# Small sums on GpSimd, attention evictions on ScalarE and two weight sums joined, in a fused attention and two-stage feed-forward kernel

## The chip, the cores and the metric

The kernel runs on one core of one Trainium2 chip. The metric is the device time of one execution in microseconds. Of the kernel before there are three timed runs and one profiled execution.

## What is computed

Three stages follow each other, all in fp32 accuracy:

```
scores = q @ k.T / sqrt(64) + alibi bias, masked to 0 <= i - j < 128
attn   = exp(scores - max) ; attn / (sum(attn) + 1e-9)     # per row
x      = attn @ v, heads side by side                      # [2304, 512]
x      = (sigmoid(x @ w_gate) * (x @ w_val)) @ w_out       # 512 -> 1536 -> 512
expert = argmax(normalised x @ normalised expert_emb.T)    # 8 experts, one each token
out    = gate * (relu(x @ w1[expert]) @ w2[expert])
```

There are 4 batches of 8 heads with 576 rows of 64. An fp32 product is made of three matmuls of split operands (high and low parts), which is why so many copies and subtractions stand beside the matmuls.

## The kernel before

The attention is cut into 36 *units*: a pair of heads on 256 rows. Five engines work on several units at once, each on its own queue, in order:

- `unit_s(i)`: TensorE writes the scores of unit i to two PSUM banks. In `tail`, VectorE reduces each of four pieces of 128x192 (line 229: adds the bias, takes the maximum) and ScalarE makes the exp of each piece with its row sum in `su` (line 232). Pieces at the ends of a sequence use an edge tile for the bias, which `make_edge` has GpSimd compute (line 160).
- `unit_n(i)`: a small instruction on 128x4 adds 1e-9 to the four sums (line 247, tile `rs`), VectorE takes the reciprocals (line 248), and GpSimd scales the four pieces with them (line 111).
- `unit_t(i)`: TensorE transposes the scaled pieces (line 261), ScalarE and VectorE copy them out (`tt`).
- `unit_b(i)`: TensorE multiplies by v (lines 283 and 289, "AV"); the two halves of 128x128 are copied from PSUM to `xf` (line 296, the eviction).

Step i of the loop issues `unit_t(i)`, `unit_b(i-1)`, `unit_n(i+2)`, `make_edge(i+5)`, `unit_s(i+3)`. Up to step 9 (`SPLIT`) TensorE, VectorE, ScalarE and GpSimd keep exactly this order; from step 10 to 20 only TensorE and GpSimd do, and a scheduler sets the order on VectorE and ScalarE; from unit 20 on all four are again in written order, and the first feed-forward stage runs between the units' pieces.

That stage takes its weights in blocks f = 0 to 11 and multiplies with seven products in place of eight for a 2x2 split (`seven`), for which `sum_x` and `sum_w` add and subtract quarters. `sum_w(f)` makes T1 = b12 - b11 and T3 = b12 - b22 (lines 363 and 364), then T2 and T4 (lines 366 and 367) on VectorE, from a block of 128 x (4 quarters of 2x128). `split_x` casts an input to its high part on ScalarE and subtracts it on VectorE (128x1024). The weights come as 64-bit words, and `conv64_a` and `conv64_b` convert them.

```python
        for i in range(SPLIT):
            if i < NA:
                unit_t(i)
            if i:
                unit_b(i - 1)()
                load_v(i + 3)
            if i < NA:
                unit_n(i + 2)
                for t in AB.get(i, []):
                    t()
                make_edge(i + 5)
                unit_s(i + LEAD)
```

Of the kernel before, what the change touches and what calls it, by code (L numbers as in the profile page):

```python
# [15 lines left out]
ALU = mybir.AluOpType  # L16
# [11 lines left out]
P = 128  # L28
# [21 lines left out]
NA = 20  # L50
# [7 lines left out]
def attn_ffn_moe(ctx: ExitStack, tc: tile.TileContext, qkd, vd, wgv, w_out, emb, tau, w1, w2, cst, ids, out):  # L58
    nc = tc.nc
# [21 lines left out]
    def slot(shape, dt, name):  # L81
        return bpool.tile(shape, dt, tag="b", name=name)
# [14 lines left out]
    def hi_copy(eng, o, i):  # L97
        if eng == "a":
            nc.scalar.copy(o, i)  # L99
        elif eng == "v":  # L100
            nc.vector.tensor_copy(o, i)
        else:
            nc.gpsimd.tensor_scalar(out=o, in0=i, scalar1=1.0, scalar2=0.0, op0=ALU.mult, op1=ALU.add)

    def scale_rows(eng, t, r):
        if eng == "a":
            nc.scalar.mul(t, t, r)
        elif eng == "v":
            nc.vector.tensor_scalar_mul(t, t, r)
        else:  # L110
            nc.gpsimd.tensor_scalar(out=t, in0=t, scalar1=r, scalar2=0.0, op0=ALU.mult, op1=ALU.add)  # L111
# [129 lines left out]
    def unit_n(i):  # L241
        if i >= NU or i in has_n:
            return
        has_n.add(i)
        p, su = fst[i]
        rs = ap.tile([P, 4], F32, tag="rs", name=f"rs{i}", bufs=4)
        nc.vector.tensor_scalar_add(rs, su, 1e-9)
        nc.vector.reciprocal(out=rs, in_=rs)  # L248
        for u in range(2):
            for j in range(2):  # L250
                scale_rows("p" if i >= 2 else "vp"[j], p[:, u, j, :], rs[:, 2 * u + j:2 * u + j + 1])
# [17 lines left out]
    def x_of(c, b, g):  # L269
        b0, nb = chunks[c]  # L270
        per = 1024 // (nb * P)
        if g % per == 0 and b == b0:
            xf[c, g // per] = slot([P, per, nb * P], F32, f"xf{c}_{g}")
        return xf[c, g // per][:, g % per, (b - b0) * P:(b - b0) * P + 256]

    def unit_b(i):
        c, b, g = units[i]
        tts, os = fst.pop(i)
        v = v_t.pop(i)
        for j in range(2):  # L280
            for u in range(2):
                c0 = j * 2 * P
                nc.tensor.matmul(os[j][u * D:u * D + D, :], v[:, j, u * D:u * D + D], tts[u][:, c0:c0 + P],
                                 start=True, stop=False, skip_group_check=True)
        for y in range(2):
            for j in range(2):
                rows, m = slice(j * 64, j * 64 + 64), 2 if j == y else 1 - j
                for u in range(2):
                    nc.tensor.matmul(os[j][u * D:u * D + D, y * 64:y * 64 + 64], v[rows, m, u * D:u * D + D],
                                     tts[u][rows, P + y * 64:P + y * 64 + 64], start=False, stop=True,  # L290
                                     skip_group_check=True)
        x = x_of(c, b, g)

        def evict():
            for j in range(2):
                hi_copy("v" if i < 11 or j and i < NA else "a", x[:, j * P:(j + 1) * P], os[j])

        return evict

# [36 lines left out]
    def flat(t):  # L336
        return t.rearrange("p a f -> p (a f)")
# [18 lines left out]
    def sum_w(f, part="01"):  # L356
        if f < KF:
            if "0" in part:
                tf[f] = slot([P, 2 * KD, P], F32, f"tf{f}")
            w, t = wf[f], tf[f]  # L360
            b11, b21, b12, b22 = (w[:, 2 * z:2 * z + 2] for z in range(4))
            if "0" in part:
                nc.vector.tensor_tensor(out=t[:, 0:2], in0=b12, in1=b11, op=ALU.subtract)
                nc.vector.tensor_tensor(out=t[:, 4:6], in0=b12, in1=b22, op=ALU.subtract)
            if "1" in part:
                nc.vector.tensor_tensor(out=t[:, 2:4], in0=b22, in1=t[:, 0:2], op=ALU.subtract)
                nc.vector.tensor_tensor(out=t[:, 6:8], in0=b21, in1=t[:, 2:4], op=ALU.subtract)
                nc.sync.dma_start(tf_d[f * P:(f + 1) * P, :], flat(t))
# [138 lines left out]
    def latest(*engines):  # L507
# [6 lines left out]
        5: [lambda: split_x("rest", xf[0, 0], "h")], 6: [lambda: split_x("rest", xf.pop((0, 0)), "l")],  # L514
        12: [bA["S1+"]], 13: [bA["A22"], lambda: load_w(0)], 14: [bA["S1"], lambda: conv_w(0, 0)],
        15: [lambda: conv_w(0, 1), lambda: load_w(1)], 16: [lambda: sum_w(0)],
        17: [bA["A11"], lambda: split_w(0, 0, 0)], 18: [bA["S3+"], lambda: split_w(0, 0, 1)],
        19: [bA["S3"], bA["S2+"], sA[0]["rg"]], 20: [bA["S2"], sA[0]["rv"]],
    }
    AB = {}  # L520
    with tc.manual_schedule(engines={ENG.PE, ENG.DVE, ENG.Activation, ENG.Pool}):
# [14 lines left out]
        load_qk(4)  # L536
        load_qk(5)
        unit_n(0)
        unit_s(2)
        keep_warm(6)  # L540
        load_qk(6)
        unit_n(1)
# [12 lines that stand above are left out]
                load_qk(i + LEAD + 4)  # L555
            for t in AT.get(i, []):
                t()
# [20 lines left out]
    def bulk(f):  # L578
        return {
            0: [lambda: load_w(f + 2), lambda: conv_w(f + 1, 0, "a")],  # L580
            1: [lambda: conv_w(f + 1, 1, "a"), lambda: conv_w(f + 1, 0, "b")],
            2: [lambda: conv_w(f + 1, 1, "b")],
            3: [lambda: split_w(0, f + 1, 0, "h"), lambda: sum_w(f + 1, "0")],
            4: [lambda: sum_w(f + 1, "1")],
            5: [lambda: split_w(0, f + 1, 0, "l")],
            6: [lambda: split_w(0, f + 1, 1, "h")],
            7: [lambda: split_w(0, f + 1, 1, "l")],
        }
# [120 lines left out]
    for f in range(KF):  # L709
        s, t = sv[f], sv[f + 1] if f + 1 < KF else None  # L710
# [528 lines left out]
```

## Time and profile before

| | |
|---|---|
| median of three runs | 831.67 us (831.55 to 832.48) |
| the profiled execution, its own time | 831.14 us |
| its span, first to last instruction | 829.4 us |
| TensorE matmuls busy | 802.5 us (97%) |
| VectorE busy | 548.6 us (66%) |
| ScalarE busy | 447.5 us (54%) |
| GpSimd busy | 176.8 us (21%) |

The profile is of one execution. Engines are named as on its page: PE is TensorE (PEld its weight loads), DVE VectorE, ACT ScalarE, POOL GpSimd, SP the queue that issues most DMAs. In a timeline a row is one instruction, or several equal ones that follow each other; in square brackets stands how long the engine had been idle before it, and what ended that. Durations overlap a little with the next instruction's start, so the spacing of starts is the better price of a short one. TensorE's busy time covers matmuls that were issued and were still waiting for something inside, so it is not time at the peak.

### The profile page before, as it was taken

What the parts mean: (1) busy time and instruction counts of PE and PEld (TensorE: products, weight loads), DVE (VectorE), ACT (ScalarE), POOL (GpSimd) and SP (SyncE); (2) the same over time, 40 slices, a digit from 0 to 9 for tenths busy, and PEclk for the clock granted to TensorE, in tenths of its full rate; (3) what the DMA queues carried; (4) which work ended last, traced back from release to release, by engine and by line L of the source; (5) the groups of instructions that cost most, each with busy time, mean ns of one, the idle gap of its engine ahead of it and who ended that gap; (6) DMA issues with size and microseconds to landing.
All of it is one profiled execution on the core that took longest, in us unless ns stands there. A gap on an engine that the chain in (4) does not pass through costs nothing. (4 is left out here: it accounts for less than half of the span.)

```text
span 829.4 us, 15487 instructions
## 1 busy us (share of the span) xinstructions
PE 802.5 (97%) x5597; PEld 657.0 (79%) x5598; DVE 548.6 (66%) x1385; ACT 447.5 (54%) x943; POOL 176.8 (21%) x263
## 2 busy tenths in 40 slices
PE   8988799999999999999999999999999999999996
PEld 5766587888888788887777777778778988978885
DVE  6999877777788888878555545547745545545443
ACT  6888666766555666568455554435334433424331
POOL 5877332322100000000010000131322030230210
PEclk9999999999999999999999999999999999999999
DMA  7686655645456486667144445142565554453510
GB/s 261 186 250 194 218 190 195 233 155 190 160 191 208 156 279 230 225 237 227 51 136 144 141 145 155 69 141 52 179 213 177 188 177 129 150 203 120 180 69 18
DMA packets 67568, 141.45 MB, mean 171 GB/s; under 512 B 8440, under 2 KB 28664, under 8 KB 67490
## 3 DMA queue, kind: packets, MB, share of 16 engines
q1 hardware_dynamic: 63586, 130.32, 48.2%
q0 software_dynamic: 3904, 10.12, 3.7%
q8 instruction: 45, 0.74, 0.4%
q14 instruction: 33, 0.27, 0.1%
HBM read 104.14 MB, written 36.93 MB: 170 GB/s over the span
## 5 line engine op out<-in xcount | busy, mean ns | idle before, releaser
L801 PE MATMUL y<-wo,gh 128*128 128x512 f32 x432 | 141.2, 402 | 0.0
L981 PE MATMUL h<-xe,weh 128*128 128x256 f32 (+4 forms) x512 | 105.9, 301 | 1.4 <-DVE h L984 1.4
L111 POOL TENSOR_SCALAR p<-p,rs 128x192 f32<-128x192 f32 x140 | 81.1, 596 | 103.5 <-DVE rs L248 49.0
L997 PE MATMUL z<-weh,h 128*128 128x512 f32 (+3 forms) x320 | 103.1, 399 | 0.0
L801 PEld LDWEIGHTS y<-wo,gh 128*128 128x128 f32 x432 | 79.9, 188 | 20.4 <-issue 3.3
L115 DVE TENSOR_TENSOR wel<-wer,weh 128x1024 fp32r<-128x1024 f32 x64 | 78.1, 1223 | 19.9 <-ACT weh L99 18.8
L981 PEld LDWEIGHTS h<-xe,weh 128*128 128x128 f32 x512 | 83.2, 188 | 4.2 <-DVE h L984 2.9
L801 PE MATMUL y<-wo,gl 128*128 128x512 f32 x216 | 85.8, 398 | 0.0
L983 ACT ACTIVATE h<-h 128x256 fp32r<-128x256 f32 (+4 forms) x64 | 26.6, 418 | 95.5 <-PE h L981 91.9
L232 ACT ACTIVATE p<-p,mx 128x192 f32<-128x192 f32 x144 | 64.1, 447 | 25.0 <-DVE mx L229 24.3
L981 PE MATMUL h<-xe,wel 128*128 128x256 f32 (+4 forms) x256 | 76.2, 299 | 0.3 <-DVE wel L115 0.2
L99 ACT CAST weh<-wer 128x1024 fp32r<-128x1024 f32 x64 | 66.2, 1048 | 8.7 <-DMA wer<-in_w 8.7
L997 PEld LDWEIGHTS z<-weh,h 128*128 128x128 f32 (+3 forms) x320 | 56.6, 180 | 15.0
L997 PE MATMUL z<-wel,h 128*128 128x512 f32 (+3 forms) x160 | 63.1, 395 | 0.0
L1002 POOL DMA_INDIRECT out<-y,cols x19 | 24.9, 1311 | 172.0 <-DVE y L1001 161.1
L1001 DVE TENSOR_SCALAR y<-z,xg 128x512 f32<-128x512 f32 (+3 forms) x22 | 16.5, 749 | 57.5 <-PE z L997 50.3
L984 DVE SCALAR_TENSOR_TENSOR h<-h,h 128x256 fp32r<-128x256 f32 (+4 forms) x64 | 29.6, 464 | 37.6 <-ACT h L983 37.3
L895 POOL DMA_INDIRECT tab_d<-ids_sb,ai x18 | 18.3, 1017 | 162.0 <-DVE ai L892 142.4
L817 ACT ACTIVATE xr<-y 128x512 f32<-128x512 f32 x18 | 10.8, 598 | 76.2 <-PE y L801 68.9
L981 PEld LDWEIGHTS h<-xe,wel 128*128 128x128 f32 x256 | 48.0, 188 | 0.7 <-DVE wel L115 0.7
L801 PEld LDWEIGHTS y<-wo,gl 128*128 128x128 f32 x216 | 40.5, 188 | 9.0
L822 DVE COPY xT<-tl 128x512 f32<-128x512 f32 x18 | 12.5, 692 | 41.5 <-PE tl L821 41.5
(332 smaller groups left out, 1940.3 us busy)
## 6 DMA issues: line engine op xcount, KB each, us to landing
wer<-in_w SPq DMA_DIRECT2D x64, 512.0 KB, 4.5
gl<-gT_d SPq DMA_DIRECT2D x27, 512.0 KB, 5.6
wr<-in_wgv SPq DMA_DIRECT2D x24, 512.0 KB, 5.2
gT_d<-c SPq DMA_DIRECT2D x48, 256.0 KB, 2.2
qk<-in_qkd SPq DMA_DIRECT2D x36, 320.0 KB, 3.4
v<-in_vd SPq DMA_DIRECT2D x36, 192.0 KB, 2.6
wf_d<-wf SPq DMA_DIRECT2D x12, 512.0 KB, 2.8
tf_d<-tf SPq DMA_DIRECT2D x12, 512.0 KB, 3.2
```

The lines of the kernel that those rows point to most:

```text
L99: nc.scalar.copy(o, i)
L111: nc.gpsimd.tensor_scalar(out=t, in0=t, scalar1=r, scalar2=0.0, op0=ALU.mult, op1=ALU.add)
L115: e.tensor_tensor(out=o, in0=i, in1=h.bitcast(F32), op=ALU.subtract)
L232: nc.scalar.activation(out=o, in_=o, func=AF.Exp, scale=-1.0, bias=mx[:, z:z + 1], accum_out=su[:, z:z + 1])
L801: nc.tensor.matmul(m, g[:, k % 4, u * P:(u + 1) * P], w[:, k % 3, :], start=(k == 0 and z == 0), stop=(k == KF - 1 and z == 2))
L895: nc.gpsimd.indirect_dma_start(out=tab_d, out_offset=IOA(ap=ai[:, u:u + 1], axis=0), in_=ids_sb[:, t:t + 1], in_offset=None)
L981: nc.tensor.matmul(m[:, :n], w[:, fs], x[:, k, :], start=(cnt == 0), stop=(cnt == 3 * KD - 1))
L983: nc.scalar.activation(out=hh, in_=m[:, :n], func=AF.Relu)
L984: nc.vector.scalar_tensor_tensor(out=hl, in0=m[:, :n], scalar=0.0, in1=hh.bitcast(F32), op0=ALU.max, op1=ALU.subtract)
L997: nc.tensor.matmul(m[0:w, :], h, ww[:, ds], start=(cnt == 0), stop=(cnt == 3 * KE - 1))
L1001: nc.vector.tensor_scalar_mul(y[0:w, :], m[0:w, :], x[0:w, DM:DM + 1])
L1002: nc.gpsimd.indirect_dma_start(out=out, out_offset=IOA(ap=idx[0:w], axis=0), in_=y[0:w, :], in_offset=None, bounds_check=NT - 1, oob_is_er ...
```

## The change

Three edits. The small sum of `unit_n` goes from VectorE to GpSimd, for all 36 units. The eviction of `unit_b` is on VectorE only for the second half (j = 1) of units 0 to 10; it was on VectorE for both halves of these and for the second half of units 11 to 19. The rest of them are on ScalarE. And `sum_w` makes T1 and T3 in one instruction of 128x512 elements, with b12 read twice, in place of two of 128x256.

```diff
@@ unit_n
         rs = ap.tile([P, 4], F32, tag="rs", name=f"rs{i}", bufs=4)
-        nc.vector.tensor_scalar_add(rs, su, 1e-9)
+        nc.gpsimd.tensor_scalar(out=rs, in0=su, scalar1=1e-9, scalar2=0.0, op0=ALU.add, op1=ALU.add)
         nc.vector.reciprocal(out=rs, in_=rs)
@@ unit_b
             for j in range(2):
-                hi_copy("v" if i < 11 or j and i < NA else "a", x[:, j * P:(j + 1) * P], os[j])
+                hi_copy("v" if j and i < 11 else "a", x[:, j * P:(j + 1) * P], os[j])
@@ sum_w
             if "0" in part:
-                nc.vector.tensor_tensor(out=t[:, 0:2], in0=b12, in1=b11, op=ALU.subtract)
-                nc.vector.tensor_tensor(out=t[:, 4:6], in0=b12, in1=b22, op=ALU.subtract)
+                w4, t4 = (y.rearrange("p (b k) c -> p b k c", b=4) for y in (w, t))
+                nc.vector.tensor_tensor(out=t4[:, 0::2], in0=w4[:, 2:3].broadcast_to([P, 2, 2, P]), in1=w4[:, 0::3],
+                                        op=ALU.subtract)
```

GpSimd's queue around unit 3, before (p_224, p_289 and p_352 are the pieces of units 2, 3 and 4; edge_0_269 and edge_2_272 the edge tiles of unit 5, edge_0_400 and edge_2_403 those of unit 7):

```order
L111 TENSOR_SCALAR p_224<-p_224,rs_262 128x192 x4
L160 TENSOR_SCALAR edge_0_269<-relm 128x192 x2
L160 TENSOR_SCALAR edge_2_272<-relm 128x192 x2
L111 TENSOR_SCALAR p_289<-p_289,rs_331 128x192 x4
L111 TENSOR_SCALAR p_352<-p_352,rs_393 128x192 x4
L160 TENSOR_SCALAR edge_0_400<-relm 128x192 x2
L160 TENSOR_SCALAR edge_2_403<-relm 128x192 x2
```

and after the change, from the edges of unit 5 on:

```order
L160 TENSOR_SCALAR edge_2_272<-relm 128x192 x2
L247 TENSOR_SCALAR rs_331<-su_291 128x4
L111 TENSOR_SCALAR p_289<-p_289,rs_331 128x192 x4
L247 TENSOR_SCALAR rs_393<-su_354 128x4
L111 TENSOR_SCALAR p_352<-p_352,rs_393 128x192 x4
L160 TENSOR_SCALAR edge_0_400<-relm 128x192 x2
L160 TENSOR_SCALAR edge_2_403<-relm 128x192 x2
L247 TENSOR_SCALAR rs_461<-su_422 128x4
```

Each sum stands right ahead of its unit's scaling, and for units 3, 5, 7 and so on behind the edges of a later unit.

VectorE's queue around the reciprocal of unit 17, in the part that the scheduler orders, before (xl_(0, 'S1') is the low part of a feed-forward input, rs_1258 the small tile of unit 17, tt_1_1237 the transposed pieces of unit 15, xf_0_1109 the attention's output):

```order
L115 TENSOR_TENSOR xl_(0, 'S1')_1222<-xq_(0, 'S1')_1083,xh_(0, 'S1')_1221 128x1024
L101 COPY xf_0_1109<-t_1_1162 128x128
L247 TENSOR_SCALAR rs_1258<-su_1210 128x4
L101 COPY tt_1_1237<-t_1_1236 128x384
L125 TENSOR_SCALAR wf_1225<-wf_1225 128x512
L248 RECIPROCAL rs_1258<-rs_1258 128x4
L229 ISA p_1279,mx_1280<-s_0_1265,bias_130 128x192
```

and after:

```order
L115 TENSOR_TENSOR xl_(0, 'S1')_1222<-xq_(0, 'S1')_1083,xh_(0, 'S1')_1221 128x1024
L248 RECIPROCAL rs_1258<-rs_1258 128x4
L101 COPY tt_1_1237<-t_1_1236 128x384
L125 TENSOR_SCALAR wf_1225<-wf_1225 128x512
L229 ISA p_1279,mx_1280<-s_0_1265,bias_130 128x192
```

The eviction and the sum are gone, and the reciprocal, which now waits for GpSimd, has moved ahead of the copy and the conversion.

## Rows read from the trace of the kernel before

**Rows 1.** Windows by stretch: span, then busy us of each engine, clock, DMA.

```profile
16.00:47.00 31.00, 29.70 (x622) 24.55 (x626) 28.09 (x146) 26.06 (x104) 25.98 (x66) 1.00 0.68 192
47.00:78.00 31.00, 25.27 (x447) 19.55 (x438) 29.51 (x114) 26.18 (x90) 22.82 (x41) 1.00 0.77 246
78.00:100.00 22.00, 17.73 (x165) 13.53 (x164) 19.51 (x44) 15.65 (x43) 9.80 (x13) 0.99 0.56 182
210.00:400.00 190.00, 189.48 (x949) 156.21 (x948) 157.84 (x234) 116.47 (x179) 1.50 (x3) 1.00 0.62 211
```

**Rows 2.** Timeline of VectorE, units 3, 4 and 13: start us, us, engine, line.

```profile
17.27 0.18 DVE L248 RECIPROCAL rs<-rs 128x4 f32<-128x4 f32 x1
17.38 0.36 DVE L229 CUSTOM_DVE_ANT_0 p<-s,bias 128x192 f32<-128x192 f32 x1
...
19.68 0.32 DVE L247 TENSOR_SCALAR rs<-su 128x4 f32<-128x4 f32 x1 [0.23 <-ACT p L232]
20.03 0.18 DVE L248 RECIPROCAL rs<-rs 128x4 f32<-128x4 f32 x1
...
45.31 0.18 DVE L248 RECIPROCAL rs<-rs 128x4 f32<-128x4 f32 x1
```

**Rows 3.** Timeline of ScalarE, unit 4: first exp, and last sum.

```profile
17.79 0.46 ACT L232 ACTIVATE p<-p,mx 128x192 f32<-128x192 f32 x1 [0.39 <-DVE mx L229]
...
19.46 0.19 ACT L232 ACTIVATION_READ_ACCUMULATOR p<-p,mx 128x1 f32 x1
```

**Rows 4.** Timeline of GpSimd, scalings and edges around units 3 to 13.

```profile
16.71 1.64 POOL L160 TENSOR_SCALAR edge<-relm 128x192 f32<-128x192 f32 x4
...
20.41 1.64 POOL L111 TENSOR_SCALAR p<-p,rs 128x192 f32<-128x192 f32 x4 [0.43 <-DVE rs L248]
22.01 1.31 POOL L160 TENSOR_SCALAR edge<-relm 128x192 f32<-128x192 f32 x4
...
31.08 2.60 POOL L111 TENSOR_SCALAR p<-p,rs 128x192 f32<-128x192 f32 x4 [0.80 <-DVE rs L248]
33.76 1.66 POOL L160 TENSOR_SCALAR edge<-relm 128x192 f32<-128x192 f32 x4
...
44.58 0.68 POOL L160 TENSOR_SCALAR edge<-relm 128x192 f32<-128x192 f32 x2
```

**Rows 5.** Groups by tile or line: duration ns min/median/max, first and last start.

```profile
L247 DVE TENSOR_SCALAR rs<-su x36: 153/165/404, 10.6 to 207.9; 128x4 f32<-128x4 f32 x36
L111 POOL TENSOR_SCALAR p<-p,rs x140: 422/429/2445, 11.1 to 210.6; 128x192 f32<-128x192 f32 x140
L160 POOL TENSOR_SCALAR edge<-relm x46: 347/353/1310, 5.4 to 163.9; 128x192 f32<-128x192 f32 x46
L99 ACT COPY xf<-t x41: 242/268/283, 47.7 to 229.6; 128x128 f32<-128x128 f32 x41
L101 DVE COPY xf<-t x31: 274/280/292, 16.4 to 80.2; 128x128 f32<-128x128 f32 x31
L363 DVE TENSOR_TENSOR tf<-wf x12: 394/423/564, 64.7 to 251.5; 128x256 f32<-128x256 f32 x12
```

**Rows 6.** Timeline of VectorE and GpSimd around the reciprocal of unit 17.

```profile
55.52 2.60 POOL L111 TENSOR_SCALAR p<-p,rs 128x192 f32<-128x192 f32 x4 [0.67 <-PE t L261]
56.05 1.36 DVE L115 TENSOR_TENSOR xl_(0, 'S1')_1222<-xq_(0, 'S1')_1083,xh_(0, 'S1')_1221 128x1024 fp32r<-128x1024 f32 x1
...
57.34 0.28 DVE L101 COPY xf<-t 128x128 f32<-128x128 f32 x1
57.54 0.20 DVE L247 TENSOR_SCALAR rs<-su 128x4 f32<-128x4 f32 x1
57.64 0.54 DVE L101 COPY tt<-t 128x384 f32<-128x384 f32 x1
...
58.20 0.84 POOL L160 TENSOR_SCALAR edge<-relm 128x192 f32<-128x192 f32 x2
...
58.75 0.16 DVE L248 RECIPROCAL rs<-rs 128x4 f32<-128x4 f32 x1
```

## The prediction

> **What bounds the kernel now.** I read the span in stretches first [rows 1]. From 210 to 400 us TensorE is busy for 189.5 of 190 us: nothing that VectorE, ScalarE or GpSimd lose or win there moves the end. Before that it is not the bound. In 16 to 47 us (units 3 to 13 of the attention) VectorE has 28.1 and ScalarE 26.1 of 31 us, each with idle in every unit, and TensorE's 29.7 include matmuls that stretch while they wait for a bank; in 47 to 78 us VectorE is the fullest, 29.5 of 31 us; in 78 to 100 us it is so again, with 19.5 of 22 us against TensorE's 17.7. Everything after runs behind TensorE, so a microsecond that the attention loses before 100 us reaches the end whole.
>
> Then I read one unit in the timelines of VectorE and ScalarE, to find the loop that sets the pace in the first stretch [rows 2, 3]. Write R(k) for the start of unit k's reciprocal. R(3) is 17.27; 0.11 later the first reduction of unit 4 starts (17.38), 0.41 after that ScalarE's first exp (17.79), and the four exps with their sums end at 19.65. VectorE has stood idle for 0.23 us and starts the small sum of unit 4 at 19.68, 0.03 after; R(4) is 20.03. The loop is 2.76 us, and 2.38 of it lie between a reciprocal and the end of the next unit's exps. VectorE idles in each turn, so what is taken off VectorE there is worth nothing; what is put into the loop is paid in full. R(13) is 45.31: ten turns took 28.04 us.
>
> Last I read GpSimd's timeline, since the sum goes there [rows 4]. It scales unit 4 at 20.41, 0.20 after that unit's reciprocal has ended, for 1.64 us, and behind units 2, 4, 6 and 8 it makes four edge tiles (1.31 to 1.66 us), later two (0.68 us) behind every second unit. Those edges are for a unit three or more ahead; today nobody waits for them but GpSimd's own next scaling.
>
> **The change, part by part.** *The small sum.* On VectorE it took 0.165 us in the median, up to 0.404 [rows 5]. On GpSimd it stands, as the order shows, behind the edges and ahead of the scaling, and the reciprocal of VectorE waits for it; behind that reciprocal wait the next unit's four reductions, its evictions, and through them ScalarE's exps and TensorE's next scores. Three prices are not in the trace. The add itself: at least VectorE's 0.165, at most the 0.353 of a GpSimd instruction with 192 columns; with four columns little but the fixed part is left, so I take 0.20, nearer to the low end. From ScalarE to GpSimd: 0.20, as from VectorE to GpSimd [rows 2, 4], at least 0.03. From GpSimd to VectorE: 0.05, near the 0.03 from ScalarE to VectorE, at most 0.20.
>
> The Trainium skill, GPSIMD Engine Reference, section "Elementwise — side-by-side cycle accounting", gives GpSimd 1.96 times VectorE's time for an add of 2048 columns and two inputs. By that ratio the add would take 0.32 us as an estimate and the sum below would be 1.3 us larger; no row here shows an add of four columns on GpSimd.
>
> So a turn without edges is 2.38 + 0.20 + 0.20 + 0.05 = 2.83 us. A turn with edges is set by GpSimd: 0.38 from the reciprocal's start to the scaling (20.03 to 20.41), 1.64 of scaling, the edges, 0.20 for the add and 0.05: 3.58 us with four edges of 1.31 in all, 2.95 with two. At unit 3 the four edges end at 18.35, so R(3) becomes 18.60, not 17.27. Then, up to unit 13: five turns without edges, 14.15; units 5 and 7, 7.16; unit 9, whose scaling of unit 8 took 2.60 beside a long VectorE subtraction and whose edges took 1.31 to 1.66, 0.38 + 2.60 + 0.08 + 1.50 + 0.25 = 4.81; units 11 and 13, 5.90. R(13) becomes 18.60 + 32.02 = 50.62: **5.3 us later**. With the low prices (0.165, 0.03, 0.03; edges 1.31) the same addition gives 49.04, 3.7 later; with an add as long as a scaling (0.429) and 0.20 for each way it gives 54.96, 9.7 later.
>
> *47 to 78 us.* Here VectorE is the bound, and relief counts. Around unit 17 [rows 6] the eviction starts 0.20 us before the sum and the sum 0.10 before the next copy: 0.30 off VectorE per unit, 2.7 us for the nine units. Against it stands the same queue. After 57.34 VectorE would go straight to the reciprocal of unit 17. GpSimd is then still scaling unit 16, which ends at 58.12 beside a subtraction of 1.36 us, and makes two edges to 59.04; with the add that is 59.3. The reciprocal stood at 58.75 today, behind a copy and a conversion that now come after it: about 1.7 us of VectorE idle in place of 0.3 saved. Units 15, 19 and 21 have edges too, in slacker places; by the same walk they give up some 0.2, 0.3 and 0.5. Relief and waits are both 2.7 us: I count **nothing**. The ends: no waits, -2.7; all four such units as unit 17, +4.1.
>
> *Evictions on ScalarE.* The diff moves more than the change's short name says: the left half of units 0 to 10 and the right half of units 11 to 19, twenty copies, 0.28 us on VectorE and 0.268 on ScalarE [rows 5]. In the first stretch ScalarE has a gap in each turn (0.39 us before 17.79, where it waits for a reduction [rows 3]), and the matmuls whose result it copies are a unit old by then: nothing. In 47 to 78 us it has 26.2 of 31 us [rows 1]; nine more copies make 28.6. That is covered while VectorE is the later of the two; around units 16 and 17, where ScalarE also casts, up to 1 us could show, inside the +4.1.
>
> *The joined sums.* One subtraction of 128x512 for two of 128x256 at 0.42 each [rows 5]: it can save 0 to 0.42, say 0.2. One lies in 47 to 78 us and is in that walk's margin; the one of block 1 lies in 78 to 100 us, with a sum off VectorE there: **-0.3** together. The other ten are covered by TensorE [rows 1].
>
> Sum: +5.3 + 0 - 0.3 = +5.0 us. The profiled execution took 831.14 us around its span of 829.4, so the new one is at 836.1; the median of the runs shown lies 0.53 above the profiled one, so the forecast is **836.5 us**.
>
> **The rivals.** *VectorE's relief wins.* If GpSimd's adds were done before their reciprocals are due, the loop of the first stretch would stay as it is and 47 to 78 us would give back its 2.7, with the -0.3 and the 0.2: 828.5. It decides at the waits before reciprocals: under 0.3 us a unit the change wins. For it: VectorE's 29.5 of 31 us. Against it: at unit 3 alone the edges end 1.08 us after the reciprocal was due [rows 2, 4]. 0.12.
>
> *It comes out even.* The low prices (+3.7) with full relief in the second stretch (-2.7, -0.3): 832.4. It needs both. 0.13.
>
> *The add is locked out.* Beside VectorE's long two-input instructions GpSimd's groups of four take 2.60 us, not 1.64 [rows 4, 6]. If in the nine units of the second stretch the reciprocal has to wait for such a stretched group each time, without the slack I gave units 16, 18 and 20, that is nine times 0.96 more: 8.6, and 845. The Trainium skill, SBUF — State Buffer, section "Who interferes with whom", has it that a VectorE instruction with two inputs in SBUF and a GpSimd instruction that reads SBUF exclude each other for their whole length; by that rule this is what would happen wherever they meet. The trace agrees as to the scaling (2.60 against 1.64). Against the rival: VectorE waits while the add is due, so nothing of its own holds GpSimd up then. 0.08.
>
> **How the numbers follow.** My own case has 0.67. A measurement of this kernel can tell some 0.2%, 1.66 us, from no change, so slower means above 833.33 and faster below 830.01. Slower: 0.67 + 0.08 = 0.75; same 0.13; faster 0.12. The ends of my own case are +0.7 (3.7 - 2.7 - 0.3), 832.4, and +13.5 (9.7 + 4.1 - 0.3), 845.2; both high ends together are unlikely, so I stop at 843. Below I go into the even case, to 831: what is left out is the faster case, a little of the even one and the far end of the lock-out.
>
> **What would show it.** Right: VectorE's idle before line 248 grows from nothing to over 5 us, released by GpSimd's line 247; the reciprocals of units 3, 5, 7 and 9 come right after edges; unit 13's stands at about 50.6 us; GpSimd's line 247 takes about 0.2 us; around unit 17 VectorE idles over 1 us. ScalarE's copies of xf would show no new wait behind them in the first stretch. Wrong: unit 13's reciprocal before 47 us, an idle before line 248 of under 2.7 us in all, or TensorE in 100 to 400 us with waits that it does not have today.

## Result, and the profile after

The changed kernel takes 839.8 us in the median of six runs (839.45 to 841.24), beside it the kernel before 831.61 (830.43 to 832.67): ratio 1.0101, 95% interval 1.0088 to 1.0114, 8.2 us slower. The forecast was 836.5 us and slower, the range 831.0 to 843.0. The profiled execution took 839.57 us, its span is 837.8.

Windows by stretch of the changed kernel, to be read against [rows 1] (line numbers from 363 on are one higher than before):

```profile
16.00:47.00 31.00, 25.42 (x500) 19.76 (x503) 19.88 (x105) 22.81 (x95) 24.05 (x65) 1.00 0.56 164
47.00:78.00 31.00, 24.68 (x470) 19.11 (x472) 23.36 (x95) 25.67 (x97) 24.24 (x50) 1.00 0.72 236
78.00:100.00 22.00, 19.44 (x237) 15.19 (x232) 19.00 (x45) 18.02 (x51) 18.49 (x27) 1.00 0.48 146
210.00:400.00 190.00, 189.50 (x994) 156.38 (x994) 156.28 (x235) 119.48 (x191) 3.53 (x6) 1.00 0.61 213
```

From 210 us on TensorE is as full as before (189.50 of 190 us). In the first two stretches TensorE, VectorE and ScalarE have less to show: VectorE falls from 28.1 to 19.9 and from 29.5 to 23.4 us. Only GpSimd has more, and only in the second (22.8 to 24.2 us). No engine is full; they wait in a circle. The waits name it (engine, line, what it waited for; us in all, times, longest):

```profile
DVE rs L248 <- POOL rs L247: 20.3, 19, 1.8
PE t L261 <- ACT xf L99: 6.7, 11, 1.6
```

The first was foretold; the second was not (it was 1.6 us in 3 waits before). Where the time is lost is read off the starts R(k) of the reciprocals, VectorE's timeline of the changed kernel, units 0, 3, 4, 5, 8, 9, 13 to 17, 22 and 24:

```profile
11.19 0.17 DVE L248 RECIPROCAL rs<-rs 128x4 f32<-128x4 f32 x1
...
18.93 0.18 DVE L248 RECIPROCAL rs<-rs 128x4 f32<-128x4 f32 x1 [1.59 <-POOL rs L247]
21.77 0.18 DVE L248 RECIPROCAL rs<-rs 128x4 f32<-128x4 f32 x1 [0.91 <-POOL rs L247]
25.36 0.18 DVE L248 RECIPROCAL rs<-rs 128x4 f32<-128x4 f32 x1 [1.46 <-POOL rs L247]
...
34.68 0.18 DVE L248 RECIPROCAL rs<-rs 128x4 f32<-128x4 f32 x1 [0.88 <-POOL rs L247]
39.66 0.18 DVE L248 RECIPROCAL rs<-rs 128x4 f32<-128x4 f32 x1 [1.67 <-POOL rs L247]
...
51.75 0.18 DVE L248 RECIPROCAL rs<-rs 128x4 f32<-128x4 f32 x1 [0.97 <-POOL rs L247]
54.75 0.18 DVE L248 RECIPROCAL rs<-rs 128x4 f32<-128x4 f32 x1 [1.01 <-POOL rs L247]
58.71 0.18 DVE L248 RECIPROCAL rs<-rs 128x4 f32<-128x4 f32 x1 [1.08 <-POOL rs L247]
62.08 0.18 DVE L248 RECIPROCAL rs<-rs 128x4 f32<-128x4 f32 x1 [0.49 <-POOL rs L247]
66.29 0.18 DVE L248 RECIPROCAL rs<-rs 128x4 f32<-128x4 f32 x1 [1.81 <-POOL rs L247]
...
90.22 0.18 DVE L248 RECIPROCAL rs<-rs 128x4 f32<-128x4 f32 x1 [1.19 <-POOL rs L247]
...
109.57 0.17 DVE L248 RECIPROCAL rs<-rs 128x4 f32<-128x4 f32 x1
```

The same of the kernel before, units 0 and 24:

```profile
10.77 0.18 DVE L248 RECIPROCAL rs<-rs 128x4 f32<-128x4 f32 x1
...
100.56 0.18 DVE L248 RECIPROCAL rs<-rs 128x4 f32<-128x4 f32 x1
```

R(3) was 17.27 and R(13) 45.31 [rows 2]. R(0), which no part of the change precedes, differs from run to run (10.2 to 11.7 us over all profiles here; 10.77 before, 11.19 after), so from here on the loss is counted from R(0). R(13) - R(0) went from 34.54 to 40.56 us, **+6.0**; R(24) - R(0) from 89.79 to 98.38, **+8.6**. After unit 24 nothing more is lost: from R(0) to the end of the span it is 8.0 us.

GpSimd's timeline of the changed kernel shows why a reciprocal is late: units 2 to 5, then 8 and 9, then 16 and 17, then 21 and 22.

```profile
16.99 1.60 POOL L160 TENSOR_SCALAR edge<-relm 128x192 f32<-128x192 f32 x4
18.67 0.23 POOL L247 TENSOR_SCALAR rs<-su 128x4 f32<-128x4 f32 x1
19.21 1.64 POOL L111 TENSOR_SCALAR p<-p,rs 128x192 f32<-128x192 f32 x4 [0.31 <-DVE rs L248]
21.51 0.23 POOL L247 TENSOR_SCALAR rs<-su 128x4 f32<-128x4 f32 x1 [0.67 <-ACT p L232]
22.12 1.63 POOL L111 TENSOR_SCALAR p<-p,rs 128x192 f32<-128x192 f32 x4 [0.38 <-DVE rs L248]
23.72 1.30 POOL L160 TENSOR_SCALAR edge<-relm 128x192 f32<-128x192 f32 x4
25.10 0.23 POOL L247 TENSOR_SCALAR rs<-su 128x4 f32<-128x4 f32 x1
...
35.02 2.59 POOL L111 TENSOR_SCALAR p<-p,rs 128x192 f32<-128x192 f32 x4 [0.38 <-DVE rs L248]
37.70 1.62 POOL L160 TENSOR_SCALAR edge<-relm 128x192 f32<-128x192 f32 x4
39.40 0.23 POOL L247 TENSOR_SCALAR rs<-su 128x4 f32<-128x4 f32 x1
...
62.42 2.67 POOL L111 TENSOR_SCALAR p<-p,rs 128x192 f32<-128x192 f32 x4 [0.38 <-DVE rs L248]
65.18 0.77 POOL L160 TENSOR_SCALAR edge<-relm 128x192 f32<-128x192 f32 x2
66.03 0.23 POOL L247 TENSOR_SCALAR rs<-su 128x4 f32<-128x4 f32 x1
...
84.50 4.73 POOL L111 TENSOR_SCALAR p<-p,rs 128x192 f32<-128x192 f32 x4 [0.38 <-PE r L459]
89.21 0.67 POOL L160 TENSOR_SCALAR edge<-relm 128x192 f32<-128x192 f32 x2
89.95 0.23 POOL L247 TENSOR_SCALAR rs<-su 128x4 f32<-128x4 f32 x1
```

Where no edges are made (21.51, unit 4) GpSimd stands idle and the add waits for ScalarE's exps. Where they are made (18.67, 25.10, 39.40, 66.03, 89.95) the add has no idle in front of it: it waits for GpSimd's own scaling and edges.

### The profile page after: what moved, and what is told of

It is laid out like the page before. It is cut to its first block, busy times and chain, and to the rows that moved or that the text cites. A ratio compares the mean times of both kernels' runs of the same rounds, so it can differ in the third digit from the quotient of the medians.

```text
span 837.8 us, 15498 instructions
## 1 busy us (share of the span) xinstructions
PE 805.7 (96%) x5597; PEld 657.4 (78%) x5598; DVE 538.5 (64%) x1317; ACT 450.8 (54%) x963; POOL 188.4 (22%) x299
## 5 line engine op out<-in xcount | busy, mean ns | idle before, releaser
L802 PEld LDWEIGHTS y<-wo,gh 128*128 128x128 f32 x432 | 79.9, 188 | 20.3 <-issue 3.3
L111 POOL TENSOR_SCALAR p<-p,rs 128x192 f32<-128x192 f32 x140 | 85.5, 627 | 29.2 <-DVE rs L248 23.3
L232 ACT ACTIVATE p<-p,mx 128x192 f32<-128x192 f32 x144 | 64.2, 448 | 31.4 <-DVE mx L229 29.5
L1003 POOL DMA_INDIRECT out<-y,cols x19 | 24.2, 1274 | 172.3 <-DVE y L1002 155.7
L218 PE MATMUL s<-qk 64*64 64x128 f32 (+2 forms) x864 | 36.6, 276 | 5.0 <-PE t L289 2.3
```

The lines of the kernel that those rows point to most:

```text
L218: nc.tensor.matmul(ss[u][y * 64:(y + 1) * 64, j * WK + d:j * WK + d + n], q[halves[u], a:a + 64], k[halves[u], a + c0:a + c0 + n], start=T ...
L232: nc.scalar.activation(out=o, in_=o, func=AF.Exp, scale=-1.0, bias=mx[:, z:z + 1], accum_out=su[:, z:z + 1])
L802: nc.tensor.matmul(m, g[:, k % 4, u * P:(u + 1) * P], w[:, k % 3, :], start=(k == 0 and z == 0), stop=(k == KF - 1 and z == 2))
L1003: nc.gpsimd.indirect_dma_start(out=out, out_offset=IOA(ap=idx[0:w], axis=0), in_=y[0:w, :], in_offset=None, bounds_check=NT - 1, oob_is_er ...
```

## The experiments

Theory **Q** (queue): the add stands in GpSimd's in-order queue behind scaling and edges, VectorE's reciprocal behind the add. Rival **E**: the evictions on ScalarE carry much of the loss. The table has the two given kernels and all twelve experiments; ratios are against runs of the kernel before on the same chip, and R is read from one profile each (that of a_add is of its slowest run, 839.66 us, with a granted clock of 0.94 in 47 to 78 us; the changed kernel's has 1.00 there). A loss in us with a range is the ratio less one, times 831.6 us.

| kernel | median us | ratio (95%) | R(13)-R(0) | R(24)-R(0) |
|---|---|---|---|---|
| before | 831.3 to 831.8 | 1 | 34.54 | 89.79 |
| changed | 839.8 | 1.0101 (1.0088 to 1.0114) | 40.56 | 98.38 |
| a_add | 838.18 | 1.0074 (1.0057 to 1.0091) | 40.31 | 97.25 |
| b_evict | 832.48 | 1.0008 (0.9999 to 1.0018) | 35.53 | 91.17 |
| c_sums | 831.43 | 0.9991 (0.9982 to 1.0001) | 34.43 | 89.70 |
| i_add_evict | 840.13 | 1.0102 (1.0080 to 1.0123) | 40.55 | 97.99 |
| e_edge_after_add | 837.47 | 1.0073 (1.0052 to 1.0093) | 39.35 | 96.01 |
| f_noedge | 833.04 | 1.0021 (1.0011 to 1.0032) | 36.60 | 91.58 |
| n_before_noedge | 830.97 | 0.9998 (0.9989 to 1.0007) | 34.23 | 90.19 |
| p_spread | 834.95 | 1.0044 (1.0029 to 1.0060) | 36.95 | 93.98 |
| l_left | 832.39 | 1.0015 (1.0006 to 1.0024) | 35.54 | 90.83 |
| m_right | 832.39 | 1.0009 (0.9999 to 1.0019) | 34.44 | 91.62 |
| d_noadd | 828.72 | 0.9965 (0.9948 to 0.9982) | 33.01 | 86.93 |
| g_noadd_sums | 828.05 | 0.9964 (0.9951 to 0.9977) | 32.94 | 86.61 |

**The three parts alone, and two together.** a_add, b_evict and c_sums each make one hunk of the diff in the kernel before; i_add_evict makes the first two.

> The small sum on GpSimd alone; evictions and weight sums as before. Theory Q (the queue: the reciprocal waits for an add that stands behind GpSimd's scaling and edges): it holds nearly the whole loss, +6.5 to +8.5 us against before, and R(13), the start of unit 13's reciprocal, is near 51.5 us against 45.3. Rival E (the evictions: ScalarE copies them late, and TensorE's transposes wait for the banks they hold, 6.7 us of such waits after the change): the add costs only +3 to +5 us.

> The evictions on ScalarE alone. Theory Q: ScalarE has room, VectorE gains 0.2 us a unit where it is the bound, so -1.5 to +0.5 us against before. Rival E: +2 to +5 us, with TensorE waiting for ScalarE's copies of xf before its transposes for several us more than before (1.6 us there).

> The joined weight sums alone. Both theories: within 0.7 us of before; one instruction of 0.69 us stands for two of 0.42, with the spacing of starts nearly the same.

> The changed kernel without the joined sums: add on GpSimd and evictions on ScalarE. The parts alone came to +6.4, +0.7 and -0.35 us, together 6.7, and the whole to +8.2. If add and evictions hinder each other: 840 or more, like the whole (the copy of a unit then comes later on ScalarE, since its exps do, and TensorE's transposes wait for it: over 5 us of waits of the transposes for ScalarE's copies). If the parts add up and the rest is the scatter of single runs: 838.5, give or take 0.7. If the joined sums make it worse in company: 838.

The add alone carries the bulk: 6.2 us by its ratio (4.7 to 7.6), just under the 6.5 to 8.5 that Q gave, above E's 3 to 5. The evictions cost 0.7 (-0.1 to 1.5), between the two theories. The joined sums give 0.7 at best guess and might give nothing. i_add_evict, at 840.13 us with 6.6 us of waits of the transposes, met the marks for an interplay; but its interval (6.7 to 10.2 us) holds the sum of the two parts, 6.9. Up to unit 13 the trace speaks against one: the evictions add 0.24 us to R(13) - R(0) beside the add and 0.99 alone. In R(24) - R(0) the three parts come to 7.46 + 1.38 - 0.09 = 8.75 us, the whole to 8.59; but the 7.46 may be too high by the clock of a_add's profile, and by their times the three parts come to 6.1 us, the whole to 8.4. Whether add and evictions hinder each other behind unit 13 stays open.

**Is it the edges in front of the add?** First their place: in the changed kernel the edges are issued behind the add, ahead of the scaling (e_edge_after_add; `unit_n` calls what it is given between reciprocal and scaling). Then they are left out from unit 5 on, with the plain bias in their place, so part of the mask at the ends of sequences is missing (f_noedge).

```diff
 e_edge_after_add
-                unit_n(i + 2)
+                unit_n(i + 2, lambda: make_edge(i + 5))
-                make_edge(i + 5)
 f_noedge, n_before_noedge
-            kind = {0: 1, 9: 1, 4: 2, 13: 2, 5: 3, 14: 3}.get(b + j)
+            kind = None if i > 4 else {0: 1, 9: 1, 4: 2, 13: 2, 5: 3, 14: 3}.get(b + j)
```

> The changed kernel, with the edge tiles made on GpSimd behind the add and ahead of the scaling, instead of ahead of the add. Theory Q (the add waits in GpSimd's queue behind scaling plus edges, and VectorE's reciprocal behind the add): the edges leave the way from scaling to add and stand in the way to the scaling alone; but they still lie between two adds on GpSimd, so a turn with four edges falls from 3.59 us at most to what add, edges and scaling take, and one in two turns does not change; the reciprocal of unit 3 falls from 18.93 back to about 17.8, that of unit 13 comes 1 to 3 us earlier than in the changed kernel (51.75), and the time is 835.5 to 838 against its 839.8. Rival (add's own length and the two hops between engines are the price, the edges only a place where it shows): gain under 1 us.

> The changed kernel without GpSimd's edge tiles from unit 5 on: those units use the plain bias, so part of the mask at the ends of sequences is left out. Theory Q: every turn of the first stretch becomes the plain turn of about 2.84 us; the reciprocal of unit 13 comes 4 to 5 us earlier than in the changed kernel (51.75, so about 47); the idle of VectorE before line 248 falls from 20.3 us by half or more; time 833 to 835.5, still above the kernel before (831.6) by the loop's 0.3 us a turn and the evictions. Rival (hops and the add's length carry the loss): gain 1 to 2 us only, 838 to 839.

Moving them gains 2.3 us, leaving them out 6.8: Q's times in both cases. One mark of the first was missed: R(3) only falls to 18.40, not 17.8, and a turn with four edges to 3.30, since moved edges delay the scaling in front of the next add. Two of the second were missed, too: the idle before line 248 falls from 20.3 only to 11.3 us, and the turns of units 8, 9 and 12 stay longer than the plain ones (3.23, 3.28 and 3.51). VectorE's timeline without edges, units 3, 4 and 13:

```profile
17.39 0.18 DVE L248 RECIPROCAL rs<-rs 128x4 f32<-128x4 f32 x1 [0.50 <-POOL rs L247]
20.23 0.18 DVE L248 RECIPROCAL rs<-rs 128x4 f32<-128x4 f32 x1 [0.32 <-POOL rs L247]
...
47.34 0.18 DVE L248 RECIPROCAL rs<-rs 128x4 f32<-128x4 f32 x1 [0.88 <-POOL rs L247]
```

R(3) is back at 17.39 and the turn is 2.84. But leaving work out proves little if the work cost something before, too. Hence the counterpart:

> The kernel before without GpSimd's edge tiles from unit 5 on; those units use the plain bias, so part of the mask at the ends of sequences is left out. It is the counterpart of the changed kernel without edges, which was 6.8 us faster than with them. If the edges cost only because VectorE's reciprocal waits behind them for the add: nothing here, R(13)-R(0) 34.2 to 34.6, time 830.5 to 831.7. If the edges cost by themselves (GpSimd beside VectorE, its scaling late for the transposes): 1 to 3 us faster, and only the rest of the 6.8 is the wait's.

Nothing: 0.9998 (0.9989 to 1.0007). The same 40 edge instructions that cost 6.8 us where a reciprocal waits behind them were free where nobody waited for GpSimd. (Its R(24) - R(0) is 0.4 us above that of before; the granted clock of that profile is 0.94 in 47 to 78 us, where before has 1.00.) Of the changed kernel's loss 1.7 us (0.9 to 2.7) are left without edges (f_noedge): the longer loop and the evictions. The last run leaves nothing out: edges behind the add, and each unit's made in two portions in two turns, those of one piece j at a time.

```diff
 p_spread, in e_edge_after_add
-                unit_n(i + 2, lambda: make_edge(i + 5))
+                unit_n(i + 2, lambda: (make_edge(i + 4, 1), make_edge(i + 5, 0)))
```

> The changed kernel with nothing left out, but each unit's edge tiles made in two portions, one in each of two turns and behind the add: two edges in every turn of the first stretch in place of four in every second. GpSimd then has 0.23 + 0.65 + 1.64 = 2.52 us to do in a turn, less than the loop's 2.84, so by theory Q no add waits for edges any more: the turns up to unit 8 are 2.84 to 2.9 us, R(13)-R(0) is 36.6 to 37.5 (39.35 with the edges only moved behind the add, 36.60 without edges), R(24)-R(0) 91.6 to 93.5, time 833 to 835 against 839.8 of the changed kernel. Rival (it is the amount of GpSimd's edge work beside VectorE, not its place in the queue): like the kernel with the edges moved behind the add, 836.5 to 838.

GpSimd's timeline in p_spread, two turns, units 7 and 8:

```profile
28.03 0.23 POOL L247 TENSOR_SCALAR rs<-su 128x4 f32<-128x4 f32 x1 [0.27 <-ACT p L232]
28.35 0.67 POOL L160 TENSOR_SCALAR edge<-relm 128x192 f32<-128x192 f32 x2
28.99 1.64 POOL L111 TENSOR_SCALAR p<-p,rs 128x192 f32<-128x192 f32 x4
30.90 0.23 POOL L247 TENSOR_SCALAR rs<-su 128x4 f32<-128x4 f32 x1 [0.27 <-ACT p L232]
```

The add is back to waiting for ScalarE; turns up to unit 8 are 2.84 to 2.87 us and R(13) - R(0) is 36.95. With all the work of the changed kernel done, the time falls by 4.9 us to 834.95 (4.7 by the ratios); order alone does that. It is still 3.7 us (2.4 to 5.0) above the kernel before. R(24) - R(0), 93.98, ends just above what was expected: from 47 us on 2.0 us stay (R(24) - R(13) is 57.03 against 54.98 without edges). No run shows why.

**What in the evictions costs.** l_left and m_right each move one half of the copies in the kernel before.

> The kernel before with only the left halves of AV's evictions of units 0 to 10 on ScalarE; the right halves of units 11 to 19 stay on VectorE. The evictions together put the reciprocal of unit 24 1.4 us later, counted from that of unit 0 (91.17 against 89.79), 1.0 of it by unit 13. If the loss comes from the turns in which ScalarE has both copies (from unit 11 on): this one shows no loss, R(13)-R(0) 34.5 and R(24)-R(0) 89.8, time 831 to 831.8. If each copy moved behind ScalarE's exps holds a bank that the transposes want: R(13)-R(0) 35.0 or more, and +0.5 to +1 us in the time.

> The kernel before with only the right halves of the evictions of units 11 to 19 on ScalarE, so that ScalarE has both copies from unit 11 on. VectorE is then relieved by 9 copies of 0.28 us, 2.5 us in all, in the stretch in which it is the fullest. If both copies behind the exps hold the bank: the turn of unit 12 takes 3.5 us instead of 2.8, R(24)-R(0) is 0.5 to 1.5 above 89.79 although VectorE is relieved, time 831.5 to 832.8. If VectorE's fullness is what sets the pace from 47 us on: R(24)-R(0) falls by 1 to 2.5 us, time 829 to 830.5.

```diff
-                hi_copy("v" if i < 11 or j and i < NA else "a", x[:, j * P:(j + 1) * P], os[j])
 l_left
+                hi_copy("v" if j and i < NA else "a", x[:, j * P:(j + 1) * P], os[j])
 m_right
+                hi_copy("v" if i < 11 else "a", x[:, j * P:(j + 1) * P], os[j])
```

My idea that only turns with both copies on ScalarE lose fell: the left halves alone lose 1.0 us by R(13), the same as all of them, and 1.2 us of the time (0.5 to 2.0). The second theory of those lines holds: up to unit 13 TensorE waits for a copy of `xf` ahead of its transposes twice in l_left, 0.68 us at 17.81 and 0.50 at 40.64, and never in the kernel before. Behind the first the turns of units 5 and 6 grow by 0.3 us each, behind the second that of unit 12 to 3.51; units 9 and 10 give 0.4 back. ScalarE's and TensorE's timelines of b_evict around unit 12:

```profile
40.56 0.26 ACT L99 COPY xf<-t 128x128 f32<-128x128 f32 x1
41.57 0.48 ACT L99 COPY tt<-t 128x384 f32<-128x384 f32 x1 [0.76 <-PE t L261]
```

```profile
40.96 0.85 PE L261 MATMUL t<-cs,p 128*128 128x128 f32 x6 [0.49 <-ACT xf L99]
```

`os` is the fourth quarter of the PSUM tile into which a unit is transposed (line 257 and below), so the copy out of it frees the bank for the transposes of a later unit. On ScalarE that copy stands behind four exps and another copy (`tt`); TensorE waits 0.49 us for it, ScalarE in turn 0.76 for the transposes, and the turn of unit 12 takes 3.51 us in place of 2.77. m_right, whose line gave 3.5 us for unit 12, has 2.77 there, as before. It shows 1.8 us more in the trace up to unit 24, although VectorE is relieved of nine copies, but 1.0009 (0.9999 to 1.0019) in time: whether the right halves cost is not settled (its profile had a clock of 0.95 in that stretch).

**The loop without the small sum.** The sum of a row has the term exp(0) = 1, so that 1e-9 changes no fp32 sum; the reciprocal can read `su` (d_noadd, from the kernel before; g_noadd_sums with the joined sums).

```diff
-        nc.vector.tensor_scalar_add(rs, su, 1e-9)
-        nc.vector.reciprocal(out=rs, in_=rs)
+        nc.vector.reciprocal(out=rs, in_=su)
```

> The kernel before without the small add: the reciprocal is taken of the exps' sums themselves (it leaves out the 1e-9, which a sum of at least 1 in fp32 does not hold). Theory Q says that the loop from one reciprocal to the next unit's sets the pace in 16 to 47 us, so 0.2 us less in it for ten units, and 0.1 a unit where VectorE is the bound, give -1.5 to -3 us. Rival T: TensorE's own work (2.5 us a unit) or ScalarE sets the pace there, and the time stays within 0.5 us.

> The kernel before without the small sum altogether (the reciprocal reads the sums of the exps directly; 1e-9 is far below the last bit of a sum that is at least 1), and with the joined sums. If the loop of the first stretch sets the time, as theory Q has it: -3.1 for the sum that is gone and -0.35 for the joined sums, 828.0 to 829, the fastest of all. Rival (only the second stretch, where VectorE is the fullest, counts): the same time, but with the reciprocal of unit 13 unchanged at 45.3 us.

VectorE's timeline of g_noadd_sums, units 3, 4 and 13:

```profile
17.01 0.17 DVE L247 RECIPROCAL rs<-su 128x4 f32<-128x4 f32 x1
19.36 0.18 DVE L247 RECIPROCAL rs<-su 128x4 f32<-128x4 f32 x1
...
43.41 0.18 DVE L247 RECIPROCAL rs<-su 128x4 f32<-128x4 f32 x1 [0.28 <-ACT p L232]
```

The turn of unit 4 is 2.35 us in place of 2.76, the ten turns from R(3) to R(13) take 26.40 us in place of 28.04; R(13) - R(0) falls by 1.6, R(24) - R(0) by 3.2. Both kernels beat both given ones; 828.05 us is the fastest, though the two can't be told apart. The rival, a gain in the second stretch alone, falls with R(13).

## Why the prediction was right, and where its sizes were off

**The mechanism held, step by step.** GpSimd's line 247 (ns: least, median, most), against the 0.20 us taken, and ScalarE's last sum of unit 4 in the timeline:

```profile
L247 POOL TENSOR_SCALAR rs<-su x36: 229/230/731, 10.1 to 216.5; 128x4 f32<-128x4 f32 x36
```

```profile
21.16 0.19 ACT L232 ACTIVATION_READ_ACCUMULATOR p<-p,mx 128x1 f32 x1
```

From the end of the exps' sum (21.35) to the add is 0.16 us (0.20 taken), from the add's end (21.74) to the reciprocal 0.03 (0.05 taken). The turns: plain 2.81 to 2.87 (2.83 forecast), with four edges 3.59 (3.58), unit 9 4.98 (4.81). R(3) is 18.93 (18.60; the start is 0.42 later). Beside unit 9, only the turns of units 11 and 12 were longer, 3.17 (2.95) and 3.15 (2.83), the latter by the evictions' wait (2.82 in a_add). By a_add the first stretch cost +5.8 us, where the sum had +5.3.

By the 1.96 that the Trainium skill (GPSIMD Engine Reference, "Elementwise — side-by-side cycle accounting") gives for a long add, the estimate for this one was 0.32 us. The measured 0.23 lies between that and the 0.20 taken; at four columns the ratio to VectorE's 0.165 is 1.4.

**The term that failed** is "Relief and waits are both 2.7 us: I count nothing". The waits were priced well in their sum: with edges R(24) - R(13) is 57.82 us, without them 54.98, so 2.8. Their places were not, so that is in part luck: unit 17 was to lose 1.7 us, and its turn is 0.85 longer with edges than without; those of units 19, 21 and 22 are 0.85, 0.58 and 0.65 longer. The relief hardly came: without edges the stretch takes 54.98 against 55.25 before, in which the joined sum and 0.4 us of the evictions lie, too (against the counterpart without edges, 55.96, it would be 1.0). The reason stands in the windows: I took VectorE for the bound of 47 to 78 us because it was busy for 29.5 of 31 us, but in the changed kernel, with 23.4, it isn't any more. Up to unit 17 the loop over GpSimd goes on: the reciprocals of units 13 to 17 all wait for the add, for 0.97, 1.01, 1.08, 0.49 and 1.81 us. For the sum, taking work off VectorE and putting its next step behind another queue are one edit; where the sum goes altogether (d_noadd), the stretch falls to 53.92. For the evictions, two thirds of the 2.7, the relief fails without GpSimd, too: b_evict and m_right leave its queue as it was, and their R(24) - R(13) is 55.64 and 57.18, with TensorE's waits for copies of `xf` in it.

**Evictions "nothing"** was a second mis-sized term. The argument was that ScalarE has a gap and that the matmuls behind the copy are a unit old. It looked at the copy's input, not at who needs the bank that it empties: +1.4 us up to unit 24 (0.7 in time, -0.1 to 1.5), and the new wait of TensorE that "what would show it" had ruled out. **Joined sums** -0.3: the trace shows -0.09, the time -0.7 (-1.5 to 0.1); one joined instruction takes 692 ns in the median against 2 x 423 [rows 5], a saving of 0.15 where 0.2 was taken.

Together: 0.5 more in the first stretch, 1.7 for the add behind it (less, if the clock of a_add's profile is part of it), 1.4 for the evictions, 0.2 for the joined sums, 3.8 us; 5.0 + 3.8 = 8.8, and the trace has 8.6. One slip lies in the recorded sum itself: 831.14 + 5.0 + 0.53 is 836.7, not 836.5.

**The rivals.** VectorE's relief and the even case both needed adds that are done before their reciprocals are due, and fell with R(3). The lock-out's condition came true, its price did not. In units 14 to 23 every group of four scalings takes 2.46 to 4.73 us (in units 15 to 23 before, 2.21 to 3.68), and the adds of units 16, 17, 19, 20, 21 and 22 follow such a group without idle. The longest is the scaling of unit 21, beside three VectorE instructions with two inputs of 128x1024; VectorE then idles for 1.19 us:

```profile
84.50 1.22 DVE L115 TENSOR_TENSOR wl<-tf,wh 128x1024 fp32r<-128x1024 f32 x1
86.46 1.42 DVE L115 TENSOR_TENSOR xl_(0, 'S3')_1576<-xq_(0, 'S3')_1507,xh_(0, 'S3')_1575 128x1024 fp32r<-128x1024 f32 x1
87.81 1.21 DVE L311 TENSOR_TENSOR xq_(0, 'S2')_1579<-xq_(0, 'S1')_1083,xf 128x1024 f32<-128x1024 f32 x1
```

Of the four scalings the first (84.50, 1.51 us) ends 0.29 us after the first of these, the last (86.80, 2.44 us) 0.22 us after the third. The Trainium skill's rule (SBUF — State Buffer, "Who interferes with whom": they exclude each other) agrees with these rows. Nine such places at 0.96 us each were priced, 8.6 us. In a_add the reciprocals of those six units wait 3.9 us in all, but the whole stretch is only 1.7 us longer than before, edges included; that VectorE makes up for the rest, with less to do there, is argued and not shown.

## What to carry to other kernels

A small instruction moved to an emptier engine costs what stands in front of it in that engine's queue, and not its own length alone: here a turn grew by 0.08 to 0.24 us where the queue was clear (units 4, 6 and 8: 2.76, 2.63 and 2.63 to 2.84, 2.87 and 2.86) and by 0.88 where four edge tiles stood ahead (units 5 and 7: 2.71 to 3.59). Before giving an engine a step of the pace-setting loop, cut its background work into portions that fit the loop's slack (0.67 us in each turn, behind the add, in place of 1.30 in every second turn ahead of it was worth 4.9 us with the same work), or better, take the step out of the loop. And ask of every copy out of PSUM not only when its input is ready but who waits for the bank.

## What the runs showed of the hardware that was not expected

A GpSimd instruction on 128x4 takes 230 ns, more than half of one on 128x192 (429 in the median for a scaling, 353 for an edge tile [rows 5]), so by a line through two of them, an estimate, nearly all of the 230 ns is a fixed part. GpSimd's group of four scalings grew from 1.64 to 4.73 us beside three long VectorE subtractions. And in the loop VectorE starts 0.03 to 0.04 us after the instruction of GpSimd or ScalarE that it waited for, while GpSimd, from unit 4 on, starts 0.15 to 0.17 us after theirs (21.35 to 21.51, and 21.95 to 22.12; 0.20 behind VectorE in most units of the kernel before).
